# Conversion of the first seven weight tiles, and their loads, spread over attention's periods

## The chip, the cores and the metric

One core of one Trainium2 chip runs the whole program. The metric is the device time of the kernel in microseconds, the median of several runs.

## The reference

What is computed is an attention layer with a position bias, and behind it two dense blocks, all in float32:

```python
scores = q @ k.T / 8 + bias            # 4 batches x 8 heads, 576 x 576, bias from a small MLP
attn = exp(scores - max); attn /= sum  # rows
x = (attn @ v)  -> [2304, 512]
x = (h - tanh(h)) @ w_out              # h = x @ w_in,  512 -> 2048 -> 512
y = (s * relu(h2)**2 + b) @ w_out2     # h2 = x @ w_in2, 512 -> 2048 -> 512
```

## The kernel before, in words

**Attention.** The work is 16 pairs (a pair of heads, a batch), each of 5 row tiles: 80 periods n = 0..79, and six more that drain the pipeline (loop of L480). A period issues, in this order, the normalisation of period n-2 (POOL, L420), the scores of n (PE, L382, into two PSUM tiles), the exponentials of n-1 (ACT, L403) and their sums (POOL, L407), the addition of the bias and the row minimum of n (DVE, L389, which is what frees the PSUM tiles of the scores), the reciprocal for n-1 (DVE, L411), the transposes of n-3 (PE, L430) and their copies to SBUF (ACT and DVE, L442 to L449), then the products with v (PE, L460), whose result DVE copies out (`xo`, L467) and SP stores (L468). At the end of a period stand the extra items: a fetch of weights, if the period is in `FT` (L506), other loads that are due, one of which is the load of q and k of pair i at period 5i-4 (L158), and then the weight ticks that `TK` lists (L510).

**Weights.** A weight tile F has two halves, (F, 0) of the first matrix and (F, 1) of the second, each 512 KB of 64-bit float data. `fetch(F)` issues the two loads from SP (L111). `weights_tick()` is a three-stage software pipeline over the halves in the order `wq`, which begins (0,0), (1,0), (0,1), (2,0), (1,1), (3,0), ...: entry 13 is (7,0) and entry 14 is (6,1). One tick runs the last stage of one half (ACT L122 rounds to the high part, POOL L87 subtracts to get the low part), the middle stage of the next (DVE L130, L142) and the first stage of the one behind (ACT L138, DVE L139). A first stage is left out when its half has not been fetched in program order. `wdone[2]` counts finished halves. Tiles 0 to 6 (`NW0 = 7`) have room of their own, tiles 7 to 15 use room that attention leaves, so they are fetched only behind it.

**Dense chunks.** Steps n run over (chunk, f): 9 chunks of rows, 16 steps each. A step first makes ticks until `wdone[2]` reaches `want` (L567, L576), with the split of the hidden tile of step n-1 after the first tick (ACT L332, DVE L333), then the first product of step n (`gemm1`, 12 matmuls, L312), its gate (ACT L322, DVE L323), and at last the second product of step n-2 (`gemm2`, 12 matmuls, L548). `gemm1` of step n needs half 2n-1 of the order, `gemm2` half 2n-2. The `gemm1` of steps 0 and 1 is issued inside attention's drain, at n = 80 and 82. Chunk 0 has 512 rows and is the one that consumes weights as they are converted. Every engine runs its instructions in program order, SP too.

Of the kernel before, what the change touches and what calls it, by code (L numbers as in the profile page):

```python
# [29 lines left out]
NW0 = 7  # L30
# [12 lines left out]

FT = {8: 0, 13: 1, 26: 2, 31: 3, 40: 4, 45: 5, 50: 6}
TK = [80 + j for j in (-11, -7, -2, 1, 2, 3, 3, 4)]
PR = [(0, 2), (2, 3)]
XPRE = [(-22, "load", 0), (-20, "hi", 0), (-19, "lo", 0), (-18, "load", 1), (-16, "hi", 1), (-15, "lo", 1),
        (-12, "load", 2), (-9, "hi", 2), (-8, "lo", 2), (-5, "load", 3), (-2, "hi", 3), (-1, "lo", 3)]  # L50
# [8 lines left out]
def tile_kernel(ctx, tc, qk, vd, wcat, wts, sb, ltab, psib, ipsi8, out):  # L59
# [48 lines left out]
    def fetch(F):  # L108
        for h in range(2):
            raw = slot(F, h, [512], I64)  # L110
            nc.sync.dma_start(out=raw, in_=wts[F, h])  # L111
            raw_w[F, h] = raw.bitcast(I32).rearrange("p (n two) -> p n two", two=2)

    def weights_tick():

        a, b_, c = wdone
        if c < b_:
            F, h = wq[c]
            x = wx_t.pop(c)[0]
            wdone[2] += 1  # L120
            w = wt[F, h] = slot(F, h, [2, 512], F32R)
            nc.scalar.copy(w[:, 0], x)  # L122
            rest(w[:, 1], x, w[:, 0])
        half = b_ < a
        if half:

            wdone[1] += 1
            x, sg = wx_t[b_]
            xi = x.bitcast(I32)
            nc.vector.scalar_tensor_tensor(out=xi, in0=xi, scalar=3, in1=sg,  # L130
                                           op0=ALU.logical_shift_left, op1=ALU.bitwise_or)
        if a < len(wq) and wq[a] in raw_w:

            wdone[0] += 1
            y = wst.tile([128, 512], F32, tag="wx", name="wx")
            sg = wsg.tile([128, 512], I32, tag="wsg", name="wsg")
            hw = raw_w[wq[a]][:, :, 1]
            nc.scalar.activation(out=y, in_=hw.bitcast(F32), func=AF.Copy, scale=2.0 ** -112)  # L138
            nc.vector.tensor_scalar(out=sg, in0=hw, scalar1=-2 ** 31, scalar2=1, op0=ALU.bitwise_and, op1=ALU.bitwise_or)  # L139
            wx_t[a] = (y, sg)  # L140
        if half:
            nc.vector.scalar_tensor_tensor(out=xi, in0=raw_w.pop(wq[b_])[:, :, 0], scalar=29, in1=xi,  # L142
                                           op0=ALU.logical_shift_right, op1=ALU.bitwise_or)
# [17 lines left out]
    def load_v(i):  # L161
        hp, b = pairs[i]
        v_t[i] = vvp.tile([128, 2, 5, D], F32, tag="vv", name="vv")
        nc.sync.dma_start(out=v_t[i], in_=vd[hp, b])
# [112 lines left out]
    def load_x(c):  # L277

        layer, c0, cn = CHUNKS[c]
        raws = {}  # L280

        def load(kk, r=None):
            if r is None:
                r = xpools["s"].tile([128, CH], F32, tag="xr", name="xr")
            raws[kk] = r[:, 0:cn]
            nc.sync.dma_start(out=raws[kk], in_=x2_d[:, kk, c0:c0 + cn] if layer else x1_d[kk][:, c0:c0 + cn])

        def hi(kk):
            if kk % 2 == 0:
                x = xpools[c % 2, kk // 2].tile([128, 2, 2, CH], F32R, tag=f"x{kk // 2}", name=f"x{kk // 2}")  # L290
                for j in range(2):
                    x_t[c, kk + j] = (x[:, j, 0, 0:cn], x[:, j, 1, 0:cn])
            rounded(x_t[c, kk][0], raws[kk])

        def lo(kk):
            rest(x_t[c, kk][1], raws.pop(kk), x_t[c, kk][0])

        return load, hi, lo
# [31 lines left out]
    def split(c, f):  # L330
        g, gh, gl = g_t[c, f]
        nc.scalar.copy(gh, g)  # L332
        nc.vector.tensor_tensor(out=gl, in0=g, in1=gh.bitcast(F32), op=ALU.subtract)  # L333


    with ExitStack() as ca:
# [20 lines left out]
        for i in range(2, len(pairs)):  # L357
            work.setdefault(5 * i - 4, []).append(lambda i=i: load_qk(i))
            work.setdefault(5 * i - 3, []).append(lambda i=i: load_v(i))
        TICKS = {n: TK.count(n) for n in TK}  # L360
        PRE = {}
# [100 lines left out]
        def emit_out(i, u):  # L462
            hp, b = pairs[i]
            r0, n = UNITS[u]
            del unit_t[i, u]
            xo = sp.tile([128, 320], F32, tag="xo", name="xo", bufs=3)[:, 0:n]
            nc.vector.tensor_copy(xo, o_t.pop((i, u)))  # L467
            nc.sync.dma_start(out=x1_d[hp][:, b * S + r0:b * S + r0 + n], in_=xo)  # L468
# [11 lines left out]
        for n in range(NK + 6):  # L480
# [20 lines left out]
            for i, u, js in PV.pop(n, []):  # L501
                for j in js:
                    emit_pv(i, u, j)
                if js[-1] == 4:
                    emit_out(i, u)
            if n in FT:  # L506
                fetch(FT[n])
            for f in work.pop(n, []):
# [10 lines left out]
    with ExitStack() as cb:  # L519
        wpools[1] = cb.enter_context(tc.tile_pool(name="wp1", bufs=1, reuse_waits="tile"))  # L520
        xb = cb.enter_context(tc.tile_pool(name="xb", bufs=1, reuse_waits="tile"))
        xpools[1, 0] = xpools[1, 1] = xb
        op_ = cb.enter_context(tc.tile_pool(name="op", bufs=3, reuse_waits="tile"))
        ps_a = cb.enter_context(tc.tile_pool(name="ps_a", bufs=1, space=PSUM, reuse_waits="tile"))

        acc = {}

        def gemm2(c, f):
            layer, c0, cn = CHUNKS[c]
            _, gh, gl = g_t.pop((c, f))  # L530
            w = wt[layer * 16 + f, 1]
            nd = KD if layer == 0 else cn // 128
            for d in range(nd):
                if f == 0:
                    acc[d] = ps_a.tile([128, 512], F32, tag=f"a{d}", name=f"a{d}")
                first, last = f == 0, f == NF - 1
                if layer == 0:
                    o = acc[d][:, 0:cn]
                    wh = w[:, 0, d * 128:d * 128 + 128]
                    wl_ = w[:, 1, d * 128:d * 128 + 128]  # L540
                    prods = ((wh, gh), (wh, gl), (wl_, gh))
                else:
                    o = acc[d]
                    wh, wl_ = w[:, 0], w[:, 1]
                    a, l = gh[:, d * 128:d * 128 + 128], gl[:, d * 128:d * 128 + 128]
                    prods = ((a, wh), (a, wl_), (l, wh))
                for j, (x, y) in enumerate(prods):
                    nc.tensor.matmul(o, x, y, start=first and j == 0, stop=last and j == 2)  # L548
            if f == NF - 1:
                for d in range(nd):  # L550
                    o = op_.tile([128, 512], F32, tag="o", name="o")
                    if layer == 0:
                        (nc.vector.tensor_copy if d % 2 else nc.scalar.copy)(o[:, 0:cn], acc[d][:, 0:cn])  # L553
                        nc.sync.dma_start(out=x2_d[:, d, c0:c0 + cn], in_=o[:, 0:cn])
                    else:
                        (nc.vector.tensor_copy if d % 2 else nc.scalar.copy)(o, acc[d])
                        r0 = c0 + d * 128
                        nc.sync.dma_start(out=out[r0:r0 + 128, :], in_=o)

        xwork = {}  # L560
        seq = [(c, f) for c in range(len(CHUNKS)) for f in range(NF)]
        LAG, LEAD = 2, 4
        swap = (NC1 - 1) * NF
        for F in range(NW0, FF):
            fetch(F)
        for n in range(len(seq) + LAG):
            want = min(32, LEAD + 2 * n)  # L567
            m = n - swap - LAG - 1
            if 0 <= m < 16:
                fetch(16 + m)  # L570
            if FF + n < 16:
                fetch(FF + n)
            if m >= 1:
                want = 32 + min(32, int(1.4 * m))
            last = [seq[n - 1]] if len(PR) < n <= len(seq) else []
            while wdone[2] < want:  # L576
                weights_tick()
                if last:
                    split(*last.pop())
            if last:  # L580
                split(*last.pop())
            if n < len(seq):
                c, f = seq[n]
                if f == XF and c + 1 < len(CHUNKS):
                    load, hi, lo = load_x(c + 1)
                    for kk in range(KD):
                        xwork.setdefault(n + 2 * kk, []).append(lambda load=load, kk=kk: load(kk))
                        xwork.setdefault(n + 2 * kk + XL, []).append(lambda fs=(hi, lo), kk=kk: [g(kk) for g in fs])
                if n >= len(PR):
                    gemm1(c, f)  # L590
                    gate(c, f)
                for g in xwork.pop(n, []):
                    g()
            if n >= LAG:
                gemm2(*seq[n - LAG])
# [57 lines left out]
```

## Time and profile before

| | |
|---|---|
| median of 3 runs | 1127.81 us (1127.48 to 1128.42) |
| the profiled execution's own time | 1128.03 us |
| its span, first to last instruction | 1126.2 us |
| mean granted TensorE clock | 0.998 |

Times in the rows are microseconds from the span's start. Engines: PE is TensorE's matmuls, PEld its weight loads, DVE is VectorE, ACT ScalarE, POOL GpSimd, SP the engine that issues the transfers. In a timeline row the bracket tells how long the engine had been idle in front of it and what ended that; durations of successive rows overlap by about 0.1 us.

### The profile page before, as it was taken

Reading aid. Unit: us, or ns where it says so; the run is one execution under the profiler, and the core shown is the slowest. Engines: PE = TensorE matmul, PEld = TensorE weight load, DVE = VectorE, ACT = ScalarE, POOL = GpSimd, SP = SyncE. Lnnn points to the kernel's source line nnn. Section 1 sums busy time; section 2 is a strip of 40 time slices with the busy share of each in tenths; the row PEclk is TensorE's granted clock in tenths of the full one; section 3 lists DMA queues with packets and bytes.
Section 4 is the critical chain, followed back from the end, with each engine's and each line's share of the span. In section 5 each row is a group of like instructions: output and inputs, shape, how many; then the busy total and the mean of one; then the engine's idle time right before and its main releaser. Section 6 shows DMA issues by size and latency. Waiting matters only on the chain.

```text
span 1126.2 us, 16944 instructions
## 1 busy us (share of the span) xinstructions
PE 1105.7 (98%) x6344; PEld 882.9 (78%) x6344; DVE 633.7 (56%) x1237; ACT 485.2 (43%) x1003; POOL 316.0 (28%) x438
## 2 busy tenths in 40 slices
PE   9999999999998899999999999999999999999998
PEld 6556566656666679999999999888888888889997
DVE  8866666667699962222232269999443343343433
ACT  8976676667655532222222244554222222222222
POOL 0155554576644642011020025635030020020000
PEclk9999999999999999999999999999999999999999
DMA  7847356453053001010020057520020020020000
GB/s 284 302 145 239 115 190 211 135 174 117 27 208 155 17 32 40 1 58 9 1 66 1 1 194 236 201 89 19 1 75 1 1 66 1 1 66 1 29 1 29
DMA packets 41043, 99.59 MB, mean 88 GB/s; under 512 B 4992, under 2 KB 14592, under 8 KB 40960
## 3 DMA queue, kind: packets, MB, share of 16 engines
q1 hardware_dynamic: 40960, 98.50, 25.6%
q8 instruction: 50, 0.82, 0.3%
q14 instruction: 33, 0.27, 0.1%
HBM read 73.41 MB, written 25.07 MB: 87 GB/s over the span
## 4 chain that ended last, share of the span: by engine, by line
PE 80%; DVE 12%; issue 3%; ACT 1%; POOL 0%; DVEq 0%; ACTq 0%
PE a L548 29%; PE h L312 29%; PE s L382 7%; PE o L460 7%; PE t L430 7%; DVE wsg L139 4%; DVE wx L130 3%; DVE ring L333 2%; DVE ring L323 1%; DVE wx L142 1%; ACT p L403 0%; DVE raw L389 0%; ACT ring L332 0%; ACT w L122 0%; DVE ring L326 0%
## 5 line engine op out<-in xcount | busy, mean ns | idle before, releaser
L312 PE MATMUL h<-x,w 128*128 128x512 f32 (+2 forms) x1920 | 425.3, 370 | 0.0
L312 PEld LDWEIGHTS h<-x,w 128*128 128x128 f32 x1920 | 357.5, 188 | 46.4 <-POOL w L87 0.7
L548 PE MATMUL a<-ring,w 128*128 128x448 f32 (+1 forms) x960 | 216.6, 372 | 12.7 <-DVE ring L333 10.8
L548 PE MATMUL a<-w,ring 128*128 128x512 f32 x864 | 210.2, 391 | 0.1
L548 PEld LDWEIGHTS a<-ring,w 128*128 128x128 f32 x960 | 179.2, 188 | 36.8 <-DVE ring L333 16.3
L548 PEld LDWEIGHTS a<-w,ring 128*128 128x128 f32 x864 | 161.6, 188 | 32.8 <-DVE o L553 0.6
L332 ACT CAST ring<-ring 128x512 fp32r<-128x512 f32 (+2 forms) x160 | 92.3, 577 | 139.9 <-DVE ring L327 100.1
L333 DVE TENSOR_TENSOR ring<-ring 128x512 fp32r<-128x512 f32 (+2 forms) x160 | 107.3, 670 | 79.5 <-ACT ring L332 79.5
L87 POOL TENSOR_TENSOR w<-wx,w 128x512 fp32r<-128x512 f32 x64 | 98.2, 1536 | 182.6 <-ACT w L122 178.5
L420 POOL TENSOR_SCALAR pn<-p,sm 128x576 f32<-128x576 f32 (+2 forms) x208 | 123.2, 609 | 76.5 <-DVE sm L411 43.6
L389 DVE CUSTOM_DVE_ANT_0 raw<-s,bias 128x576 f32<-128x576 f32 x144 | 103.9, 754 | 64.7 <-PE s L382 56.7
L326 DVE TENSOR_TENSOR ring<-ring 128x512 f32<-128x512 f32 (+1 forms) x80 | 52.9, 662 | 148.7 <-ACT ring L325 148.7
L323 DVE TENSOR_TENSOR ring<-h,ring 128x448 f32<-128x448 f32 (+1 forms) x80 | 50.7, 634 | 146.1 <-ACT ring L322 146.1
L84 POOL TENSOR_SCALAR x<-xr 128x448 fp32r<-128x448 f32 (+2 forms) x36 | 25.7, 713 | 347.9 <-DMA xr<-x_d 347.9
L325 ACT ACTIVATE ring<-h 128x512 f32<-128x512 f32 (+1 forms) x80 | 44.3, 554 | 159.1 <-PE h L312 159.1
L322 ACT ACTIVATE ring<-h 128x448 f32<-128x448 f32 (+1 forms) x80 | 44.2, 553 | 157.6 <-PE h L312 157.6
L403 ACT ACTIVATE p<-raw,mn 128x576 f32<-128x576 f32 x144 | 110.7, 772 | 1.2 <-DVE mn L389 0.8
L430 PEld LDWEIGHTS t<-ident,pn 128*128 128x128 f32 (+1 forms) x656 | 69.8, 140 | 32.6 <-issue 18.1
L460 PE MATMUL o<-pt,vv 128*64 128x256 f32 (+1 forms) x640 | 95.0, 418 | 0.0
L382 PE MATMUL s<-qk 64*128 64x288 f32 (+1 forms) x640 | 91.5, 429 | 1.0 <-DVE mn L389 1.0
L430 PE MATMUL t<-ident,pn 128*128 128x128 f32 (+1 forms) x656 | 89.5, 279 | 0.7 <-DVE pt L442 0.6
L442 ACT COPY pt<-t 128x384 f32<-128x384 f32 x128 | 61.2, 479 | 66.0 <-PE t L430 66.0
(46 smaller groups left out, 783.3 us busy)
## 6 DMA issues: line engine op xcount, KB each, us to landing
w<-in_wts SPq DMA_DIRECT2D x64, 512.0 KB, 4.6
qk<-in_qk SPq DMA_DIRECT2D x16, 864.0 KB, 7.0
bias_d<-m SPq DMA_DIRECT2D x36, 296.0 KB, 4.3
bias<-bias_d SPq DMA_DIRECT2D x32, 288.0 KB, 4.5
vv<-in_vd SPq DMA_DIRECT2D x16, 320.0 KB, 3.2
out_x<-o SPq DMA_DIRECT2D x18, 256.0 KB, 2.1
xr<-x_d SPq DMA_DIRECT2D x16, 224.0 KB, 2.6
x_d<-o SPq DMA_DIRECT2D x16, 224.0 KB, 2.0
```

The source lines that it names most:

```text
L87: nc.gpsimd.tensor_tensor(out=lo, in0=raw, in1=hi.bitcast(F32), op=ALU.subtract)
L312: nc.tensor.matmul(h, a, x, start=(k == 0), stop=(k == 3 * KD - 1))
L323: nc.vector.tensor_tensor(out=g, in0=h, in1=t, op=ALU.subtract)
L332: nc.scalar.copy(gh, g)
L333: nc.vector.tensor_tensor(out=gl, in0=g, in1=gh.bitcast(F32), op=ALU.subtract)
L382: nc.tensor.matmul(o[:, c, 0:288], q[h, ee, t * 128:t * 128 + n], kk[h, ee], start=True, stop=True)
L389: nc.vector.tensor_tensor_reduce(out=raw.rearrange("p (c j) -> p c j", c=2), in0=s_t.pop((x, j))[:, :, 0:288], in1=bias_t[pairs[i][0], k]. ...
L403: nc.scalar.activation(out=p, in_=raw, func=AF.Exp, scale=-1.0, bias=mn, accum_out=sm[:, j:j + 1])
L420: nc.gpsimd.tensor_scalar(out=pn[:, c:c + b - a], in0=p[:, a:b], scalar1=sm[:, j:j + 1], scalar2=0.0, op0=ALU.mult, op1=ALU.add)
L430: nc.tensor.transpose(pm[0:c, j - g], pn[:, j * 128:j * 128 + c], ident)
L460: nc.tensor.matmul(o[h], v[:, e, j], unit_t[i, u][:, 4 if j == 4 else 5 * e + j, 0:n], start=(j == 0), stop=(j == 4))
L548: nc.tensor.matmul(o, x, y, start=first and j == 0, stop=last and j == 2)
```

## The change

The fetches of tiles 0 to 6 come every sixth period from 4 to 40 in place of the periods 8 to 50. The list of ticks has 16 in attention (periods 15, 19, ... 59, then 66, 70, 74, 78) in place of 3 there (69, 73, 78) and 5 in the drain (81 to 84). In the dense chunks the count of halves that a step waits for starts from 13 and rises by 1.3 a step, in place of 4 and 2 a step; from step 13 on the old rule is the larger one.

```diff
-FT = {8: 0, 13: 1, 26: 2, 31: 3, 40: 4, 45: 5, 50: 6}
-TK = [80 + j for j in (-11, -7, -2, 1, 2, 3, 3, 4)]
+FT = {4 + 6 * F: F for F in range(7)}
+TK = [*range(15, 63, 4), 66, 70, 74, 78]
...
         for n in range(len(seq) + LAG):
-            want = min(32, LEAD + 2 * n)
+            want = min(32, max(LEAD + 2 * n, 2 * NW0 - 1 + int(1.3 * n)))
```

## Rows read from the trace of the kernel before

**Rows 1.** The page, part 1: busy time, share of the span, instructions.

```profile
PE 1105.7 (98%) x6344; PEld 882.9 (78%) x6344; DVE 633.7 (56%) x1237; ACT 485.2 (43%) x1003; POOL 316.0 (28%) x438
```

**Rows 2.** Busy time by stretch (PE, PEld, DVE, ACT, POOL, granted clock): attention, chunk 0.

```profile
57.96:284.20 226.24, 226.24 (x1696) 136.49 (x1695) 145.68 (x453) 159.71 (x411) 128.07 (x262) 1.00 0.50 165
315.16:409.31 94.15, 81.87 (x338) 63.22 (x337) 92.11 (x113) 47.06 (x83) 51.06 (x37) 0.98 0.30 112
330.06:403.21 73.15, 63.14 (x265) 48.70 (x264) 73.15 (x89) 37.06 (x66) 41.42 (x28) 1.00 0.29 110
```

**Rows 3.** Groups of DVE instructions in 330.06 to 403.21 (eleven steps): busy us, mean ns.

```profile
L139 DVE TENSOR_SCALAR wsg<-w 128x512 int32<-128x512 int32 x22 | 33.3, 1514 | 0.0
L142 DVE SCALAR_TENSOR_TENSOR wx<-w,wx 128x512 int32<-128x512 int32 x22 | 16.0, 728 | 0.0
L130 DVE SCALAR_TENSOR_TENSOR wx<-wx,wsg 128x512 int32<-128x512 int32 x22 | 16.0, 728 | 0.0
L323 DVE TENSOR_TENSOR ring<-h,ring 128x512 f32<-128x512 f32 x12 | 8.1, 677 | 0.0
L333 DVE TENSOR_TENSOR ring<-ring 128x512 fp32r<-128x512 f32 x11 | 7.5, 679 | 0.0
```

**Rows 4.** Waits in the same stretch: us in total, times, longest.

```profile
PE a L548 <- DVE ring L333: 10.0, 11, 1.5
```

**Rows 5.** The chain that ended last: start, us, what; twelve matmuls without a wait.

```profile
417.07 2.73 PE a L548 x12
```

**Rows 6.** Timeline of PE at the start of chunk 0, and one window's granted clock.

```profile
322.20 1.24 PE L548 MATMUL a<-ring,w 128*128 128x512 f32 x3 [1.91 <-DVE xo L467]
323.24 4.26 PE L312 MATMUL h<-x,w 128*128 128x512 f32 x12
...
323.00:324.00 1.00, 1.00 (x4) 0.80 (x3) 1.00 (x3) 0.00 (x0) 0.00 (x0) 0.50 1.08 245
```

**Rows 7.** SP's timeline behind attention, and landing of its first three loads there.

```profile
322.59 16.30 SPq L111 DMA_DIRECT2D w<-in_wts  x18
...
DMA to landing us min/median/max: 3.8/4.6/5.4
```

**Rows 8.** Timelines of DVE and POOL around the tick of period 73.

```profile
279.95 1.08 DVE L130 SCALAR_TENSOR_TENSOR wx<-wx,wsg 128x512 int32<-128x512 int32 x1
280.95 0.43 DVE L139 TENSOR_SCALAR wsg<-w 128x512 int32<-128x512 int32 x1
281.29 1.11 DVE L142 SCALAR_TENSOR_TENSOR wx<-w,wx 128x512 int32<-128x512 int32 x1
...
279.74 2.84 POOL L420 TENSOR_SCALAR pn<-p,sm 128x576 f32<-128x576 f32 x3 [0.37 <-DVE sm L411]
```

**Rows 9.** Timelines of DVE and PE: bias additions of periods 65, 72, 73, and the scores behind.

```profile
252.68 0.76 DVE L389 CUSTOM_DVE_ANT_0 raw<-s,bias 128x576 f32<-128x576 f32 x1 [0.19 <-PE s L382]
275.48 0.76 DVE L389 CUSTOM_DVE_ANT_0 raw<-s,bias 128x576 f32<-128x576 f32 x1 [1.24 <-PE s L382]
277.99 0.75 DVE L389 CUSTOM_DVE_ANT_0 raw<-s,bias 128x576 f32<-128x576 f32 x1
...
255.19 1.24 PE L382 MATMUL s<-qk 64*128 64x288 f32 x8
277.12 1.24 PE L382 MATMUL s<-qk 64*128 64x288 f32 x8
280.65 0.71 PE L382 MATMUL s<-qk 64*64 64x288 f32 x8
```

**Rows 10.** Load of pair 4's q and k: issue, landing; its first scores; the weight loads.

```profile
96.59 0.54 SPq L158 DMA_DIRECT2D qk<-in_qk  x1
...
DMA to landing us min/median/max: 7.2/7.2/7.2
...
106.44 1.24 PE L382 MATMUL s<-qk 64*128 64x288 f32 x8
...
w<-in_wts SPq DMA_DIRECT2D x64, 512.0 KB, 4.6
```

## The prediction

> **What bounds the kernel now.** I began with the shares of the page: PE is busy 98% of the span and DVE 56% [rows 1], which looks as if DVE did not matter. A share is an average over stages, so the second view was busy time by stretch. Over 14 pairs of attention PE is busy for all 226.24 us, with 145.68 us of DVE, 159.71 of ACT and 128.07 of POOL beside it [rows 2]: PE sets the pace, 16.16 us a pair. The second stretch runs from the `gemm1` of step 2 to that of step 16, fourteen steps of chunk 0. There DVE is busy for 92.11 of 94.15 us and PE for 81.87 [rows 2]: in chunk 0 the bound is DVE. The third view, DVE's groups in eleven of these steps, shows nothing in front of which DVE was idle (73.15 us busy of 73.15) [rows 2, 3], and the fourth shows PE waiting eleven times, 10.0 us, for the split L333 [rows 4].
>
> What a step costs on DVE: 22 halves were converted in 73.15 us. A half is 1.51 + 0.73 + 0.73, less 0.08 of overlap for each, so 2.73 us; gate and split are 0.68 + 0.68 less the overlaps, 1.2 us [rows 3]. Two halves and 1.2 make 6.66 us a step, and 73.15 / 11 is 6.65. PE would need two groups of twelve matmuls at 2.73 us [rows 5], 5.46 a step.
>
> **The change, part by part.**
>
> *Fewer halves in chunk 0.* Counted from the code, the drain and steps 1 to 14 converted 32 - 1 halves (one was finished in attention). Afterwards 13 are finished in attention, and 19 are left for steps 1 to 14, one in most steps and two in about every third. DVE's mean step becomes 19/14 x 2.73 + 1.2 = 4.9 us, under PE's 5.46; a step with two halves (6.66) is caught up in the next (3.93). So PE sets the pace, and the fourteen steps fall from 94.15 [rows 2] to 28 x 2.73 = 76.4 us [rows 5]: **17.7 us gained**. The bound on the gain is the same number, since PE's own work does not change.
>
> *A pipeline that starts anew.* The list of ticks has 16 entries, but entry 13 of the order is half (7,0), which is fetched behind attention. The fourteenth and fifteenth ticks only finish what is under way, the sixteenth does nothing, and 13 halves are done. At step 1 three ticks have to run for one half, and the first of them waits on ACT and on DVE for the load of (7,0); what is queued behind it is the gates and splits of steps 2 and 3. Let T be the end of attention's last product. DVE's copy `xo` takes until T + 0.5, SP stores it and issues the loads 0.4 later (322.20 to 322.59 [rows 6, 7]), and the first lands 3.8 us on [rows 7]: T + 4.8. Behind that DVE has a first half (1.65 undisturbed, worked out below, and 0.65 of waiting for ACT's pass over the same 128 x 512, an estimate by DVE's own), three ticks of 2.73 and a gate and a split: 2.3 + 8.2 + 1.2 = 11.7, so the split of step 2 ends at T + 16.5. PE gets there with five groups of 2.73 and one matmul, T + 13.9. **2.6 us lost.** Before, a wait of 1.91 us in nearly the same place was followed by twelve matmuls in 4.26 us in place of some 2.85, with the granted clock at 0.50, the lower of the two levels [rows 6], while the eleven waits of at most 1.5 us left it at 1.00 [rows 2, 4]. So 1.4 us come on top, and the term is **4.0 lost**. Bounds: 1.5 if the ticks run as short as in rows 8 and the clock stays up, 5.5 if a load is a microsecond later. The wait of 1.91 us and its clock lie inside the 94.15 and need no term of their own.
>
> *Twelve more ticks in attention.* By shares there is room: thirteen halves of 2.73 add 35 us to DVE's 145.68 in a stretch of 226 [rows 2]; ACT and POOL have 66 and 98 us idle there, five or more for each half, of which they run two instructions and one. None of them becomes the bound. What counts is delay within a period. A tick stands in front of the next bias addition on DVE, and until that has read the scores, PE can't write the next ones. The room, counted as DVE's idle time in front of the addition plus the time from its end (about 0.68 after its start) to the scores that need the buffer, is 0.19 + 1.83 = 2.0 us when the tick is at n = 4 modulo 5, 1.24 + 0.96 = 2.2 at 1, and 0 + 1.98 = 2.0 at 2 [rows 9]. At 0 and 3 I count it as ample: the tick of period 73 was at 3, and PE held its 16.16 a pair [rows 2]. How long does a tick hold DVE? Undisturbed 0.65 + 0.34 + 0.65 = 1.65 (rows 3 for the two, rows 8 for L139). At period 73 it held it 2.37 us, from 279.95 to the end of L142, with POOL's normalisation stretched to 2.84 [rows 8]; in chunk 0 it is 2.73 beside L87 [rows 3]. DVE and POOL stretched each other there.
>
> The Trainium skill ("SBUF — State Buffer", Who interferes with whom) says that a DVE instruction with two SBUF inputs, or in a two-port mode, and a GpSimd instruction that reads SBUF block each other for the whole instruction. The trace agrees: 2.37 and 2.73 us in place of 1.65. If it meant that every tick at a tight place is caught by the normalisation and by L87, the attention term below would be 11.0 and the sum 1125.8; by the rows it is 3.8 and 1118.6.
>
> Ticks with all DVE work at the tight places, from the list: 19, 39, 59 (4), 31, 51, 66 (1), 27, 47 (2). Midway between the two rows, 2.55 us a tick, the excess over the room is 0.55 x 3 + 0.35 x 3 + 0.55 x 2 = **3.8 us lost**. Bounds: 0 at 1.65, and at 3.45 (both disturbances in one tick) 1.45 x 3 + 1.25 x 3 + 1.45 x 2 = 11.0. I take the middle because a full tick has L87 beside it, but not always while DVE works.
>
> *The loads.* The fetch of tile 2 moves to period 16, where SP issues it in front of pair 4's q and k. That load was issued at 96.59 and landed 7.2 us later, 103.8; its scores begin at 106.44 [rows 10], 2.65 us of room. If it waits for one weight load of 4.6 us [rows 10], scores are 2.0 late; if the transfers share the engines as they do, 0. I take **0.5 lost**, nearer to 0 because the room of 2.65 us is used up first. The other six fetches stand at periods in which no load is due soon; their cover is that q, k and v are issued a pair ahead.
>
> **The sum.** 1128.03 - 17.7 + 4.0 + 3.8 + 0.5 = 1118.6 for the profiled execution, which was 0.2 above the median; against the median, **1118.4 us**. What is late next is PE itself in every stage.
>
> **Rivals.** (1) *Attention hides all of it.* DVE's ticks fall into its idle time, POOL's L87 between two normalisations; only the restart stays: 1128 - 17.7 + 1.5 to 4.0, so 1112 to 1114. For it: 80 us of idle DVE in the stretch [rows 2]. Against: the room of 2.0 us at three of five places [rows 9]. (2) *Attention takes most back*: 11.0 in place of 3.8, and 5.5 at the restart, 1126 at the end. (3) *Slower, by blocking between DVE and POOL.* Each tick's three DVE instructions meet the normalisation and L87 in turn, L87 stands in front of the next normalisation on POOL, and the transposes wait as well as the scores. It decides from (17.7 - 4.0) / 12 = 1.15 us a tick; if all twelve cost 1.6 us, 19 us are lost and the kernel ends at 1133. For it: 2.84 us for the normalisation at period 73 [rows 8]. Against: at that period PE lost nothing. The skill's rule above is this mechanism; by it alone the size stays open. (4) *The change moves the wait only*: chunk 0 stays late because tiles 7 to 15 land late or the restart repeats, and the time is within 0.2%. Against: 18 loads were issued within 16.3 us [rows 7], well ahead of the steps.
>
> **How the numbers follow.** My forecast, 1114 to 1123, has 0.62; rival 1 has 0.16, rival 2 with what lies between 1123 and 1125.5 has 0.13, rival 4 has 0.04, rival 3 has 0.05. Within 0.2% (2.3 us, about what a measurement of this kernel can tell from no change) means above 1125.5: faster 0.91, same 0.04, slower 0.05. The range leaves out the top of rival 2, rivals 3 and 4, and a little below: 1111 to 1124.
>
> **What would show it.** PE's waits for L333 in chunk 0 almost gone, and `gemm1` of step 16 some 14 us sooner behind that of step 2; one wait of 2 to 3 us at the second product of step 2 with a granted clock of 0.5 behind it; pairs of attention that take 16.16 us where no tick falls and up to 1 us more where one does, with scores waiting for L389. I am wrong if attention's pairs grow by over a microsecond each, if the first half behind attention is not what DVE waits for, or if chunk 0 stays at 6.6 us a step.

## The result and the profile after

The changed kernel takes 1116.35 us (1115.87 to 1117.34, four runs) where the kernel before takes 1127.85: a ratio of 0.9899, interval 0.9882 to 0.9916. The forecast was 1118.4, with 1111 to 1124 as the range. The profiled execution took 1117.34 us, the longest of the four, with a span of 1115.2. Two kernels below (loads alone, late restart) had one execution each at more than twice the time of the others, which moves their medians by 0.2 us at most and enters no ratio.

The same two stretches as in [rows 2], by busy time in the kernel after (columns as there), are attention's 14 pairs and the fourteen steps of chunk 0:

```profile
58.67:289.27 230.60, 227.81 (x1695) 135.95 (x1694) 174.21 (x488) 171.99 (x435) 150.68 (x273) 1.00 0.48 159
319.60:398.27 78.67, 76.88 (x338) 63.09 (x337) 69.35 (x86) 37.92 (x66) 35.86 (x27) 1.00 0.35 134
```

Chunk 0 fell from 94.15 to 78.67 us, 15.5 gained, and DVE is no longer its bound: 69.35 us busy of 78.67. Attention grew from 226.24 to 230.60, 4.4 lost. Two small pieces remain: attention's drain, which lost its five ticks, is 0.6 shorter, and pair 1 began 0.7 later (58.67 in place of 57.96), ahead of anything that the change does there. The rest of the program is the same to 0.1 us. -15.5 + 4.4 - 0.6 + 0.7 is -11.0, the difference of the spans.

The timeline of PE in chunk 0 after shows one place with a wait (two matmuls, 0.24 and 1.55 us) in place of the eleven waits of [rows 4], at the second product of step 2:

```profile
333.74 0.50 PE L548 MATMUL a<-ring,w 128*128 128x512 f32 x1 [0.24 <-ACT ring L332]
335.79 2.80 PE L548 MATMUL a<-ring,w 128*128 128x512 f32 x11 [1.55 <-DVE ring L333]
```

DVE's timeline names the reason; the first row is the first stage of half (7,0), the second the split on which PE waited:

```profile
324.27 0.43 DVE L139 TENSOR_SCALAR wsg<-w 128x512 int32<-128x512 int32 x1 [4.06 <-DMA w<-in_wts]
...
335.06 0.68 DVE L333 TENSOR_TENSOR ring<-ring 128x512 fp32r<-128x512 f32 x1
```

In attention the waits of PE for the row minimum, five times from the first pair on, are new; one of the two biggest stands at the scores of period 29, which need the buffer that the addition behind the tick of period 27 frees:

```profile
PE s L382 <- DVE mn L389: 2.8, 5, 0.8
```

```profile
136.78 0.72 PE L382 MATMUL s<-qk 64*64 64x288 f32 x8 [0.79 <-DVE mn L389]
```

These waits are 2.8 of the 4.4 us. The other 1.6 count as busy time of PE (227.81 in place of 226.24), since a group of matmuls that is held up inside is shown as one longer piece: the eight of the scores behind the tick of period 39 take 1.44 us in place of 1.24.

```profile
176.74 1.44 PE L382 MATMUL s<-qk 64*128 64x288 f32 x8
```

DVE's timeline at four ticks, of periods 19 (4 modulo 5; its first two stages only, so no L87 on POOL), 27 (2 modulo 5), 31 (1 modulo 5) and 39 (4 modulo 5); of the last two only the first instruction and the addition behind:

```profile
107.67 0.68 DVE L130 SCALAR_TENSOR_TENSOR wx<-wx,wsg 128x512 int32<-128x512 int32 x1
108.27 0.42 DVE L139 TENSOR_SCALAR wsg<-w 128x512 int32<-128x512 int32 x1
108.60 0.68 DVE L142 SCALAR_TENSOR_TENSOR wx<-w,wx 128x512 int32<-128x512 int32 x1
109.21 0.75 DVE L389 CUSTOM_DVE_ANT_0 raw<-s,bias 128x576 f32<-128x576 f32 x1
...
133.25 1.40 DVE L130 SCALAR_TENSOR_TENSOR wx<-wx,wsg 128x512 int32<-128x512 int32 x1
134.57 0.41 DVE L139 TENSOR_SCALAR wsg<-w 128x512 int32<-128x512 int32 x1
134.91 1.15 DVE L142 SCALAR_TENSOR_TENSOR wx<-w,wx 128x512 int32<-128x512 int32 x1
135.98 0.74 DVE L389 CUSTOM_DVE_ANT_0 raw<-s,bias 128x576 f32<-128x576 f32 x1
...
146.45 0.68 DVE L130 SCALAR_TENSOR_TENSOR wx<-wx,wsg 128x512 int32<-128x512 int32 x1
...
149.08 0.75 DVE L389 CUSTOM_DVE_ANT_0 raw<-s,bias 128x576 f32<-128x576 f32 x1
...
173.88 0.72 DVE L130 SCALAR_TENSOR_TENSOR wx<-wx,wsg 128x512 int32<-128x512 int32 x1
...
175.94 0.74 DVE L389 CUSTOM_DVE_ANT_0 raw<-s,bias 128x576 f32<-128x576 f32 x1
```

From the first instruction of a tick to the bias addition behind it, the undisturbed tick holds DVE for 109.21 - 107.67 = 1.54 us, the full one of period 27 for 135.98 - 133.25 = 2.73, as in chunk 0 [rows 3], that of period 31 for 2.63 and that of period 39 for 2.06.

### The profile page after: what moved, and what is told of

Same layout as the page of the kernel before. It is cut to its first block, busy times and chain, and to the rows that moved or that the text cites. A ratio compares the mean times of both kernels' runs of the same rounds, so it can differ in the third digit from the quotient of the medians.

```text
span 1115.2 us, 16901 instructions
## 1 busy us (share of the span) xinstructions
PE 1101.4 (99%) x6344; PEld 882.0 (79%) x6344; DVE 632.3 (57%) x1237; ACT 484.6 (43%) x1003; POOL 317.6 (28%) x438
## 4 chain that ended last, share of the span: by engine, by line
PE 84%; DVE 8%; issue 2%; DMA 0%; ACT 0%; SPq 0%; DVEq 0%
PE a L548 32%; PE h L312 32%; PE o L460 7%; PE s L382 7%; PE t L430 7%; DVE wx L130 2%; DVE wsg L139 2%; DVE wx L142 1%; DVE ring L333 1%; DVE raw L389 1%; DVE ring L323 1%; DMA w<-in_wts 0%; DVE pt L442 0%; DVE xo L467 0%; DVE ring L326 0%
## 5 line engine op out<-in xcount | busy, mean ns | idle before, releaser
L548 PE MATMUL a<-ring,w 128*128 128x448 f32 (+1 forms) x960 | 212.9, 370 | 2.3 <-DVE ring L333 2.0
L87 POOL TENSOR_TENSOR w<-wx,w 128x512 fp32r<-128x512 f32 x64 | 94.7, 1480 | 207.2 <-ACT w L122 193.3
L420 POOL TENSOR_SCALAR pn<-p,sm 128x576 f32<-128x576 f32 (+2 forms) x208 | 129.2, 637 | 44.0 <-DVE sm L411 30.6
L382 PE MATMUL s<-qk 64*128 64x288 f32 (+1 forms) x640 | 92.5, 431 | 3.8 <-DVE mn L389 3.8
```

The costliest lines, as they stand in the source:

```text
L87: nc.gpsimd.tensor_tensor(out=lo, in0=raw, in1=hi.bitcast(F32), op=ALU.subtract)
L382: nc.tensor.matmul(o[:, c, 0:288], q[h, ee, t * 128:t * 128 + n], kk[h, ee], start=True, stop=True)
L420: nc.gpsimd.tensor_scalar(out=pn[:, c:c + b - a], in0=p[:, a:b], scalar1=sm[:, j:j + 1], scalar2=0.0, op0=ALU.mult, op1=ALU.add)
```

## The experiments

**Loads alone, and ticks alone.** The change has two parts; each was run without the other.

```diff
-FT = {8: 0, 13: 1, 26: 2, 31: 3, 40: 4, 45: 5, 50: 6}
+FT = {4 + 6 * F: F for F in range(7)}
```

> The kernel before with the seven fetches moved to periods 4, 10, ... 40 and nothing else. My theory: the loads were hidden before and are hidden now, the gain lies in the conversions alone, so 1127.9 us, within 0.1% of the kernel before. Rival: the earlier loads free the transfer queues later on and carry part of the gain, 1122 us or less. A load of q and k that is delayed by the fetch at period 16 would show as up to 2 us more.

Measured: 1127.86 us, ratio 0.9998 (0.9988 to 1.0007). Stretches of this kernel:

```profile
57.16:283.39 226.23, 226.23 (x1695) 136.43 (x1694) 145.61 (x453) 159.54 (x411) 127.42 (x262) 1.00 0.49 163
314.34:408.54 94.20, 80.65 (x338) 62.00 (x337) 92.16 (x113) 46.97 (x83) 51.05 (x37) 1.00 0.29 112
```

The counterpart is the changed kernel with the old line of `FT`.

> The changed kernel with the seven fetches back at their old periods 8 to 50. My theory: 1116.4 us, the same as the changed kernel within 0.1%, since each half still lands before its first stage. Rival (loads matter): nearer to the kernel before, 1120 us or more.

Measured: 1116.09 us, ratio 0.9895 (0.9878 to 0.9911), with 230.60 us of attention and 78.98 of chunk 0. The loads carry nothing; the ticks and the slower count carry all of it.

**Where a tick stands.** Two kernels, each with all ticks at one place of the pair:

```diff
-TK = [*range(15, 63, 4), 66, 70, 74, 78]
+TK = [*range(8, 80, 5)]            # 3 modulo 5
```

> The changed kernel with its ticks at periods 8, 13, ... 78, all at 3 modulo 5, where the bias addition behind a tick has the most room. Theory of the room: attention's 14 pairs fall from 230.6 back to 226.2 us, and the time is 1116.35 - 4.4 = 1112.0 us. Rival (a tick costs its 0.34 us wherever it stands, by the blocking between DVE and POOL): no change, 1116.4 us.

```diff
-TK = [*range(15, 63, 4), 66, 70, 74, 78]
+TK = [*range(12, 78, 5), 78]       # 2 modulo 5
```

> The changed kernel with its ticks at periods 12, 17, ... 77 (and an empty or half-empty one at 78), all at 2 modulo 5. Theory of the room: the two full ticks there cost 0.87 us each in the changed kernel, and eleven full ticks cost 9.6 in place of 4.4, so 1121.5 us, with scores waiting 0.8 us for the row minimum once a pair. Rival (place does not matter): 1116.4 us.

Measured: 1112.71 us at 3 modulo 5 (ratio 0.9866, 0.9851 to 0.9880) and 1124.81 at 2 modulo 5 (0.9970, 0.9959 to 0.9982). Attention's 14 pairs and chunk 0 at 3 modulo 5:

```profile
57.65:283.89 226.24, 226.24 (x1695) 136.44 (x1694) 175.13 (x486) 170.74 (x434) 149.00 (x272) 1.00 0.49 161
314.26:394.66 80.40, 78.47 (x338) 64.24 (x337) 69.74 (x86) 37.98 (x66) 35.73 (x27) 0.98 0.34 132
```

and attention at 2 modulo 5, by stretch and by waits:

```profile
58.95:294.89 235.94, 227.07 (x1695) 136.46 (x1694) 174.85 (x486) 167.47 (x433) 153.57 (x272) 1.00 0.47 154
```

```profile
PE s L382 <- DVE mn L389: 8.8, 11, 0.8
```

DVE is busy for 175 us in both, and the same halves are converted. At 3 modulo 5 this costs PE nothing, to the hundredth of a microsecond of the kernel before; at 2 modulo 5 it costs 9.7, eleven waits. The ticks are hardly shorter where they cost nothing: most of those at 3 modulo 5 hold DVE for 2.63 us from their first instruction to the addition behind, as that of period 18 does.

```profile
101.80 0.68 DVE L130 SCALAR_TENSOR_TENSOR wx<-wx,wsg 128x512 int32<-128x512 int32 x1
...
104.43 0.74 DVE L389 CUSTOM_DVE_ANT_0 raw<-s,bias 128x576 f32<-128x576 f32 x1
```

The 9.6 of the expectation held for the stretch; its total was 3.3 us low. Of these, 1.8 are the drain (the last product ended 32.1 us behind the stretch, in place of 30.3), by the profile: behind the ticks of periods 77 and 78 PE waited there 0.54 us for the row minimum of DVE (at 308.12) and 0.94 for its copy of the transposes (at 313.16). The rest lies in small pieces and in the microsecond by which the changed kernel's profiled execution was longer than its median. At 3 modulo 5 chunk 0 took 1.7 us more than after; its clock is told of below.

**The restart.** The first tick of the dense part at step 3:

```diff
-            want = min(32, max(LEAD + 2 * n, 2 * NW0 - 1 + int(1.3 * n)))
+            want = min(32, max(2 + 2 * n, 2 * NW0 - 1 + int(1.46 * (n - 2)) if n > 2 else 0))
```

> The changed kernel with the first tick of the dense part moved from step 1 to step 3, at 1.46 halves a step with a lead of 2 over the old rule: the split of step 2 then stands behind one first stage in place of three ticks and a wait for a load. My theory: the wait of 1.8 us at the second product of step 2 goes (2.4 us with the first matmul), DVE's mean of 5.2 us a step stays under PE's 5.46, so 1116.35 - 2.3 = 1114.0 us. Rival: the restart is only moved, and the same 2 us appear two or three steps later, 1116.4 us.

Measured: 1113.57 us, ratio 0.9872 (0.9852 to 0.9892). Chunk 0 of this kernel:

```profile
318.37:394.68 76.31, 76.31 (x339) 63.17 (x338) 68.98 (x86) 37.94 (x66) 38.35 (x27) 1.00 0.36 139
```

PE has no wait left in it: 76.31 us is the 28 x 2.73 = 76.4 of the prediction, the floor. The 2.4 us (78.67 - 76.31) were the restart, and they did not appear again later.

**The rate.** Two halves a step from the start:

```diff
-            want = min(32, max(LEAD + 2 * n, 2 * NW0 - 1 + int(1.3 * n)))
+            want = min(32, 2 * NW0 - 1 + 2 * n)
```

> The changed kernel with two halves a step in the dense part from the start (32 at step 10) in place of 1.3. The same 13 halves are done in attention. My theory (what counts is DVE's time per step against PE's 5.46 us): nine to ten steps cost 6.66 us on DVE, about 1.2 us over PE's each, so some 11 us come back, 1127 us, at least 1123. Rival (what counts is how many halves are left for chunk 0, 19 x 2.73 + 14 x 1.2 = 69 us of DVE in 76 of PE): no change, 1116.4 us.

Measured: 1128.61 us, ratio 1.0006 (0.9996 to 1.0015): the whole gain is gone, though attention still does its thirteen halves. Chunk 0, and its waits in PE's timeline:

```profile
318.53:409.68 91.15, 80.39 (x338) 64.02 (x337) 69.09 (x86) 38.00 (x66) 36.70 (x27) 0.96 0.30 116
```

```profile
338.23 0.80 PE L548 MATMUL a<-ring,w 128*128 128x512 f32 x1 [5.80 <-ACT ring L332]
340.26 4.44 PE L548 MATMUL a<-ring,w 128*128 128x512 f32 x11 [1.24 <-DVE ring L333]
344.54 2.90 PE L312 MATMUL h<-x,w 128*128 128x512 f32 x12
...
359.69 2.81 PE L548 MATMUL a<-ring,w 128*128 128x512 f32 x11 [0.70 <-DVE ring L333]
...
379.86 2.79 PE L548 MATMUL a<-ring,w 128*128 128x512 f32 x11 [1.46 <-DVE ring L333]
```

DVE's busy time in the chunk is 69.09 us, as after (69.35): its sum is not what counts. The size was right, 12.5 us more than after in the chunk, but its make-up was not the one expected. I had put it down to nine steps at 1.2 us. More than half is the restart, 7.0 us of waiting with two more ticks in front of the split of step 2, and a lower clock behind it (0.50, the third number from the end):

```profile
338.00:343.00 5.00, 3.54 (x8) 2.46 (x9) 5.00 (x7) 1.94 (x5) 2.28 (x2) 0.50 1.03 410
```

The product behind the restart begins 26.0 us into the chunk (344.54 - 318.53), where it is 18.8 after (338.43 - 319.60): 7.2 of the 12.5. The steps that follow add four waits of 0.7 to 1.5 us.

**Both remedies together.**

> Ticks at 3 modulo 5 together with the late restart. If both theories hold and their gains add: 1116.35 - 4.4 - 2.3 = 1109.7 us, and PE then has hardly a wait left from the first full pair to the end of chunk 0. If place and restart don't matter: 1116.4 us.

Measured: 1109.18 us (1108.80 to 1110.74), ratio 0.9836 (0.9822 to 0.9851), faster than both kernels. Its stretches:

```profile
59.11:285.35 226.24, 226.24 (x1695) 136.44 (x1694) 175.13 (x486) 170.78 (x434) 149.00 (x272) 1.00 0.49 162
315.72:392.02 76.30, 76.30 (x338) 63.17 (x337) 69.61 (x86) 37.92 (x66) 37.64 (x27) 1.00 0.37 139
```

Both gains add, and PE is busy throughout in both stretches.

**POOL's part in a tick.** In attention alone:

```diff
-            rest(w[:, 1], x, w[:, 0])
+            if wpools[1] is None:
+                nc.gpsimd.memset(w[:, 1].bitcast(F32), 0.0)
+            else:
+                rest(w[:, 1], x, w[:, 0])
```

> The changed kernel with L87, POOL's subtraction, replaced by a fill with zeros for the thirteen halves converted in attention; the low parts of these halves are left out of the computation. DVE's three instructions of a tick stay. Theory (L87 and the normalisations hold DVE up because both engines read SBUF): a tick holds DVE 1.5 to 2.4 us in place of 2.73, most of the excess over the room of 2.0 goes, attention's 14 pairs fall from 230.6 to 226.2 to 228, so 1112.0 to 1113.8 us. Rival (it is DVE's own work and the order of the instructions that makes the scores late, not POOL): 230.6 us and 1116.4 us.

Measured: 1114.70 us, ratio 0.9885 (0.9869 to 0.9902), 0.9 above the upper end of the theory's time. The profiled execution, 1113.49 us with a span of 1111.4, was the shortest of the four. By its timeline of PE the scores of periods 5 and 75, the two ends of attention's stretch, begin at

```profile
57.63 1.24 PE L385 MATMUL s<-qk 64*128 64x288 f32 x8
...
285.43 1.24 PE L385 MATMUL s<-qk 64*128 64x288 f32 x8
```

so the stretch is 227.80 us: of the 4.4 us that attention lost, 2.8 hang on L87 in this execution. The medians differ by 1.7 only; the start of pair 1 alone moves a time by a microsecond, so the stretch is the cleaner measure. The tick of period 27 holds DVE for 2.03 us (132.22 to 134.25) in place of 2.73. (The edit adds three lines, so L385 is the L382 of the kernel after.) The edit changes more than one thing: the fill also waits for nothing on ACT, so it ran ahead of the tick's DVE work rather than beside it. That POOL's L87 lengthens the tick is shown; whether because it reads SBUF, or by where and how long it ran, is not separated.

## Why the prediction was right

*The bound.* Right. The first product of step 16 moved 15.5 us nearer to that of step 2, and the rate of two a step took 12.5 of it back with the same sum of DVE's work: what counts is how much of it falls into one step, against PE's 5.46 us, and what stands in front of a split that PE needs. The rate showed both, the second for the larger part.

*The gain of 17.7 in chunk 0.* Right as a floor: with the restart gone the chunk takes 76.31 us.

*The restart, 2.6 lost and 1.4 for the clock.* The wait was there, at the place and for the reason given; it cost 2.4 us. The load landed at T + 4.67 (324.27 - 319.60) against T + 4.8, whose own terms add up to 4.7; the upper bound of 5.5 should likewise have been 5.0, for a load a microsecond later. The 1.4 us for the clock were wrong in the profiled execution: the step that failed is to add them for certain because a wait of 1.91 us had once been followed by a lower clock. The windows around the wait, each with the granted clock as the third number from the end, in the kernel before, with the loads alone (the same wait, 1.90 us), after (1.55 us), and with the ticks at 3 modulo 5 (1.54 us):

```profile
322.00:326.00 4.00, 3.79 (x10) 2.98 (x11) 4.00 (x7) 1.32 (x3) 1.73 (x2) 0.59 0.68 200
```

```profile
321.00:325.00 4.00, 3.60 (x16) 2.98 (x17) 4.00 (x7) 1.50 (x3) 1.72 (x2) 1.00 0.64 198
```

```profile
335.00:339.00 4.00, 3.21 (x14) 2.66 (x15) 4.00 (x7) 1.97 (x4) 1.30 (x1) 1.00 1.02 409
```

```profile
330.00:334.00 4.00, 3.40 (x10) 2.70 (x11) 4.00 (x6) 2.18 (x4) 1.29 (x1) 0.68 1.03 408
```

The rows of PE with the wait in front, with the loads alone and at 3 modulo 5:

```profile
321.40 0.97 PE L548 MATMUL a<-ring,w 128*128 128x512 f32 x3 [1.90 <-DVE xo L467]
```

```profile
330.60 4.37 PE L548 MATMUL a<-ring,w 128*128 128x512 f32 x11 [1.54 <-DVE ring L333]
```

The clock fell once and not the other time behind the same wait. One occurrence in one profile was no price for every execution. The size was right where it did fall behind the restart: at 3 modulo 5 the eleven matmuls took 4.37 us in place of 2.80 after, 1.6 more, and chunk 0 took 1.7 more. In the kernel before it cost the chunk nothing (94.15 us with it, 94.20 without it, with the loads alone), since DVE was the bound there.

*Attention, 3.8 lost.* 4.4 measured. The mechanism, scores that wait for a bias addition held up by a tick, is shown by the two kernels that differ in the place of the ticks alone. The size was nearly right by two errors that cancel. PE's delay behind a tick, read from the starts of the scores against the kernel before, was 0.87 us at 2 modulo 5 (forecast 0.55), 0.71 at 1 (0.35) and 0.26 at 4 (0.55, three times; period 19 cost nothing, having no L87). 2 x 0.87 + 3 x 0.71 + 2 x 0.26 = 4.4. One length of 2.55 us for all ticks was the weak step: the rows above give 2.73 at period 27, 2.63 at 31 and 2.06 at 39. With these lengths and the rooms of the prediction the excess is 0.73, 0.43 and 0.06, which leaves 0.1 to 0.3 us of each delay over; so the rooms were counted a little too large as well. With the measured lengths the account of the room puts the places in the right order; it does not give the sizes to a tenth of a microsecond.

*The loads, 0.5 lost.* Nothing was lost, but by little. SP's issue of pair 4's q and k, its landing and the first scores in the kernel after:

```profile
98.41 0.38 SPq L158 DMA_DIRECT2D qk<-in_qk  x1
```

```profile
DMA to landing us min/median/max: 8.5/8.5/8.5
```

```profile
107.14 1.24 PE L382 MATMUL s<-qk 64*128 64x288 f32 x8
```

It landed at 106.9; of the room of 2.65 us [rows 10] 0.2 is left.

*The sum.* Forecast were -17.7 + 4.0 + 3.8 + 0.5 = -9.4 us; between the two profiled executions it was -17.8 + 2.4 + 4.4 + 0, with -0.6 from the drain and +0.7 from the start of pair 1, which is the -11.0 of the spans but for rounding. The clock's 1.4 is the largest of the differences.

*Not counted:* the drain's 0.6. The start of pair 1, 57.2 to 59.1 us in the profiles shown here, moves a total by a microsecond either way, so small effects are read from stretches.

*Rival 1* (attention hides all of it) is what the kernel with ticks at 3 modulo 5 does. *Rival 2* (attention takes most back) needed 11.0 us of attention, of which 4.4 came; its own terms give 1127 and not 1126 us. *Rival 3* (slower, from 1.15 us a tick) stayed out of reach even at the worst place tried, where eleven full ticks cost 0.88 each. *Rival 4* (the wait only moves) is out for this change by the 15.5 us of chunk 0, though the kernel with two halves a step ended at that time.

## What to carry to other kernels

Work moved under a stage whose engines have idle time in sum still has to fit into the idle time between two particular instructions: find, for each place where it could go, the idle time in front of the next instruction on its engine plus the room until the consumer needs that, and put it where this is largest. A software pipeline that runs dry restarts with all its stages in front of other work in the same queues; restart it behind the work that is due, not before it. And judge a stage by its time per step against the other engine's, and by what stands in front of work that is due, not by sums over the chunk.

## What had not been expected of the hardware

The granted clock fell to the lower of its two levels behind a wait of 1.91 us in one execution and stayed at the higher one behind 1.90 us in another, with the same instructions around it; it fell behind 1.54 us in a third and stayed behind 1.55 in a fourth. The same kernel goes both ways: of 15 executions of the kernel before, taken together with those of the loads alone, 7 had a mean granted clock of 1.000 and 8 of 0.998, the mean of the profiled one. What decides it is open.
